# Rings of 8 and 12 slots, value products eleven tiles behind, tile 3 of each head transposed by DMA

## The chip, the cores and the metric

The kernel runs on one core of one Trainium2 chip. The metric is the device time of one execution in microseconds (us), from the first to the last instruction of the program with what the runtime puts around it. Three runs of the kernel before gave 1611.88, 1615.55 and 1622.05 us; the median, 1615.55 us, is the time to compare with.

## The reference

A conditioned transformer block on 2048 rows of 640 features: an attention part with 32 heads against a given K and V cache of 2048 rows per head, then a mixer and an MLP. Only the attention part is touched by the change.

```python
def _A_ref(x, k_cache, v_cache, wq, wo):            # x (1, 2048, 640), H, Dh = (32, 128)
    q = (x @ wq).reshape(B, Sq, H, Dh).transpose(0, 2, 1, 3)
    scores = jnp.einsum('bhqd,bhkd->bhqk', q, k_cache) * Dh ** (-0.5)
    p = _softmax(scores, axis=-1)
    o = jnp.einsum('bhqk,bhkd->bhqd', p, v_cache)
    return o.transpose(0, 2, 1, 3).reshape(B, Sq, H * Dh) @ wo
...
mod = (_silu(c) @ w_mod).reshape(c.shape[0], 6, 1, -1)
h = _layernorm(x, axis=-1) * (1 + ca) + sa
x = x + ga * _A_ref(h, A_k_cache, A_v_cache, A_wq, A_wo)
h = _layernorm(x, axis=-1) * (1 + cb) + sb
x = x + gb * _B_ref(h, B_w1, B_w2, B_w3, B_w4)
```

## The kernel before

A helper class records every operation with the keys that it reads and writes, works out the semaphore waits, and emits each engine's instructions in the order in which they were recorded. So every engine's queue is in order, and the order is written out by hand.

**The main loop** (lines 506 to 583) runs over steps `s`. There are `NG` = 512 tiles: 32 heads (`h`) of 16 tiles of 128 query rows (`j` is the tile within its head). In step `s` the engines are given this work:

- TensorE (PE): `qk(s, half)` (line 286), the scores of tile `s` against all 2048 keys, in two halves of two matmuls into the PSUM banks `Sps`; right behind each half, half of `pv(g_, half)` (line 299), the product of probabilities and values for tile `g_ = s - PVD`, eight tiles back. Further, one of the pieces of the next head's Q projection (`q_piece`, line 237), and, for tiles 3 and 10 of each head, a transpose of the probabilities on TensorE (`t_piece`, line 253: 4 transposes a half-step, 16 a tile).
- VectorE (DVE): line 546, twice a tile: it takes 1024 scores out of PSUM, scales them into `negS` (three slots) and keeps the row minimum. POOL joins the two minima (line 556).
- ScalarE (ACT): line 559, the exponential of all 2048 scores into slot `s % RP` of `Pb`, as bf16. It also copies finished outputs out of PSUM (line 537, once for two tiles), the Q pieces (line 244, four a head), and the transposed tiles of TensorE (`t_evac`, line 262; half of tile 3 goes through VectorE instead, line 264).
- SP issues the DMAs. `transpose(g, n)` (line 222) transposes one or two neighbouring tiles of `Pb` into `PTs`, where `pv` reads them as weights. A pair is taken where both tiles go by DMA, so the issues of a head are, by tile, (0,1), (2), (4,5), (6,7), (8,9), (11), (12,13), (14,15): fourteen tiles in eight DMAs. Between them on the same queue stand the next head's K (a transposing load, line 205, at `j == 2`), Wq (line 209, `j == 6`) and V (line 214, `j == PVD + 1` = 9).
- POOL normalises finished tiles `LAG` = 4 steps after their product (lines 440 and 447) and writes them to a scratch tensor in DRAM (line 454, once for four tiles).

`Pb` and `PTs` are the two halves of one tensor `ring` with 2 x `RP` = 20 slots of 128 x 2048 bf16 (512 KB each): 10 for the probabilities, 10 for their transposes. The exponential of tile `s` has to wait until the tile that last used its slot has been read (by its DMA or by TensorE), and a DMA transpose until its slot of `PTs` was read by `pv`.

Ahead of the loop stands a prologue (modulation, LayerNorm, the first Q). Behind it, the output projection, mixer and MLP (lines 584 to 801) reuse the same memory; the change does not alter their instructions.

Of the kernel before, what the change touches and what calls it, by code (L numbers as in the profile page):

```python
# [6 lines left out]
ACT = mybir.ActivationFunctionType  # L7
BF16 = mybir.dt.bfloat16
# [107 lines left out]
def bass_adaLN_cond__mha_block_cached__mixer_s_mlp__prompt_kernel(  # L116
    nc, A_x, A_k_cache, A_v_cache, A_wq, A_wo, B_x, B_w1, B_w2, B_w3, B_w4, c, w_mod, out,
):
    _, SQ, D = A_x.shape
    _, H, SK, DH = A_k_cache.shape  # L120
    FF = B_w3.shape[1]
    assert DH == 128 and D % 128 == 0 and SQ % 512 == 0 and SK == 2048
    KT = D // 128
    NQT = SQ // 128
    NQC = SQ // 512
    NKT = SK // 128
# [5 lines left out]
    NG = H * NQT  # L132
# [5 lines left out]
    with ExitStack() as es:  # L138
# [3 lines left out]
        ident = sb("ident", [128, 128], BF16)  # L142
# [7 lines left out]
        if True:  # L150
            with ExitStack() as es1:
                sb1 = lambda name, shape, dt: es1.enter_context(nc.sbuf_tensor(name, shape, dt))
                RP = 10
                PVD = 8
                PE_TILES = (3, 10)
                US = KT * (SQ + 4)
                sb1("pad", [128, 32], F32)
                ring = sb1("ring", [128, 2 * RP, SK], BF16)
                negS = sb1("negS", [128, 3, SK], F32)
                wo = sb1("wo", [128, H, D], BF16)  # L160
                kv = sb1("kv", [128, 2 * SK + 2 * NKT * 130 + 2 * KT * 128 + 2 * SQ], BF16)
# [7 lines left out]
                nm0, nm1, nm, rl = [small[:, 4 * NQT + 8 * i:4 * NQT + 8 * i + 8] for i in range(4)]  # L169
# [5 lines left out]
                Vaug = kv[:, o1:o2].rearrange("p (b k d) -> p b k d", b=2, k=NKT)  # L175
                wq = kv[:, o2:o3].rearrange("p (b k d) -> p b k d", b=2, k=KT)
                QT = kv[:, o3:o3 + 2 * SQ].rearrange("p (b q) -> p b q", b=2)
                Pb = ring[:, 0:RP]
                PTs = ring[:, RP:2 * RP].rearrange("p r (k q) -> p r k q", k=NKT)
                flat = ring[:].rearrange("p r s -> p (r s)")  # L180
                XO = SK
                x_sb = flat[:, XO:XO + NQT * D].rearrange("p (t d) -> p t d", t=NQT)
                WO_ = 6 * SK
                wmod = flat[:, WO_:WO_ + KT * 2 * D].rearrange("p (k n) -> p k n", k=KT)
                RO = 13 * SK
# [6 lines left out]
                CO = SO + NQT * 24  # L192
# [1 line left out]
                mcol = flat[:, CO + 2 * KT:CO + 6 * KT].bitcast(F32)  # L194
                c_sb = flat[:, CO + 6 * KT:CO + 7 * KT]
                s_col = flat[:, CO + 7 * KT:CO + 8 * KT]
                assert CO + 8 * KT <= 2 * RP * SK and XO + NQT * D <= WO_ and WO_ + KT * 2 * D <= 10 * SK
                PO = PTp[:].bitcast(F32)
                JB = [Oaug[:, 0:512], QPp[:, 0:512]]
                JBb = [Oaug[:].bitcast(BF16), QPb]  # L200
# [13 lines left out]
                    G.dma("sync", lambda e: e.dma_start(Vaug[:, hb, :, 0:128], A_v_cache[0, h].rearrange("(t p) d -> p t d", p=128)),  # L214
                          ("v", hb), w=[("V", hb)])

                assert RP % 2 == 0 and NQT % 2 == 0
                is_pe = lambda g: g % NQT in PE_TILES

                def transpose(g, n):  # L220
                    b = g % RP
                    G.dma("sync", lambda e: e.dma_start_transpose(
                        PTs[:, b:b + n].rearrange("p r k q -> p (r k) q"), ring[:, b:b + n].rearrange("p r s -> p (r s)")),
                        ("t", b), r=[("Pb", b + i) for i in range(n)], w=[("PT", b + i, z) for i in range(n) for z in range(2)])
                jbank = [0]
                bank_of = {}

# [19 lines left out]
                def t_piece(g, r, q):  # L247
                    jb = bank(("t", g, r))

                    def f(t):  # L250
                        for z in range(4 * q, 4 * q + 4):
                            kt = 8 * r + z
                            ins = t.transpose(JBb[jb][:, z * 128:(z + 1) * 128], Pb[:, g % RP, kt * 128:(kt + 1) * 128], ident[:])
                        return ins
                    G.op("tensor", f, r=[("Pb", g % RP)], w=[("J", jb)])

                def t_evac(g, r):
                    jb = bank(("t", g, r))
                    dst = PTs[:, g % RP, r * 8:(r + 1) * 8, :]
                    src = JBb[jb].rearrange("p (k q) -> p k q", k=8)  # L260
                    if not by_dve(g, r):
                        G.op("scalar", lambda a: a.copy(dst, src), r=[("J", jb)], w=[("PT", g % RP, r)])  # L262
                    else:
                        G.op("vector", lambda v: v.tensor_copy(dst, src), r=[("J", jb)], w=[("PT", g % RP, r)])

                by_dve = lambda g, r: r == 1 and g % NQT == PE_TILES[0]

                taken = [u for j in PE_TILES for u in range(2 * (j + 3), 2 * (j + 5))]
                QPIECE = {}
# [21 lines left out]

                def pv(g, half):
                    hb = (g // NQT) % 2
                    b = g % RP
                    ob = PO[:, ((g // 2) % 2) * 512 + (g % 2) * 130:]

                    def f(t):
                        for kt in range(half * 8, half * 8 + 8):
                            ins = t.matmul(ob[:, 0:129], PTs[:, b, kt, :], Vaug[:, hb, kt, 0:129],  # L299
                                           start=(kt == 0), stop=(kt == NKT - 1))  # L300
                        return ins
                    G.op("tensor", f, r=[("PT", b, half), ("V", hb), "ones"], w=[("O", (g // 2) % 2)])

                ringk = lambda a, b: [k for i in range(a // SK, -(-b // SK)) for k in (
                    [("Pb", i)] if i < RP else [("PT", i - RP, 0), ("PT", i - RP, 1)])]
                WMK = ringk(WO_, WO_ + KT * 2 * D)
                WRK = ringk(RO, 2 * RP * SK)
                XK = [ringk(XO + cc * 4 * D, XO + (cc + 1) * 4 * D) for cc in range(NQC)]

                def load_x(cc):  # L310
# [149 lines left out]
                XB0 = XT0 + NQT * D  # L460
                GT0 = XB0 + NQT * D * 2
                NFT4 = NFT * 512
                assert GT0 + NFT4 <= 2 * RP * SK
                tmp = flat[:, 0:4 * D].bitcast(F32).rearrange("p (b d) -> p b d", b=2)
                xt = flat[:, XT0:XT0 + NQT * D].rearrange("p (t d) -> p t d", t=NQT)
                xb = flat[:, XB0:XB0 + 2 * NQT * D].bitcast(F32).rearrange("p (t d) -> p t d", t=NQT)
# [36 lines left out]
                        + ringk(XT0 + 4 * cc * D, XT0 + 4 * (cc + 1) * D))  # L503

                LAG = 4
                for s in range(NG + PVD + LAG):
                    h, j = divmod(s, NQT)
                    g_ = s - PVD
                    evacs = []
                    if s <= 2:  # L510
                        for i in ((0,), (1, 2), range(3, len(MROW)))[s]:
# [5 lines left out]
                    for half in range(2):  # L517
                        if s < NG:
                            qk(s, half)
                        if 0 <= g_ < NG:  # L520
                            pv(g_, half)
                        if s == 0 and half == 1:
                            q_head0(NQC - 1)
                        if h + 1 < H and 2 * j + half in QPIECE:
                            cc, q = QPIECE[2 * j + half]
                            q_piece(h + 1, cc, q)
                            if q == KT - 1:
                                evacs.append((q_evac, h + 1, cc))
                        for r in range(2):
                            g = s - 3 - r  # L530
                            if 0 <= g < NG and is_pe(g):
                                t_piece(g, r, half)
                                if half == 1:
                                    evacs.append((t_evac, g, r))
                    if 0 <= g_ < NG and g_ % 2 == 1:
                        p = g_ // 2
                        G.op("scalar", lambda a, p=p: a.copy(  # L537
                            Of[:, p % 4].rearrange("p z d -> p (z d)")[:, 0:259], PO[:, (p % 2) * 512:(p % 2) * 512 + 259]),
                            r=[("O", p % 2)], w=[("Of", p % 4)])
# [15 lines left out]
                    if s < NG:  # L555
                        G.op("gpsimd", lambda g, r8=r8: g.tensor_scalar(  # L556
                            out=nm[:, r8:r8 + 1], in0=nm0[:, r8:r8 + 1], scalar1=nm1[:, r8:r8 + 1], scalar2=None, op0=ALU.min),
                            r=[("nmh", 0, r8), ("nmh", 1, r8)], w=[("nm", r8)])
                        G.op("scalar", lambda a, s=s, r8=r8: a.activation(  # L559
                            Pb[:, s % RP, :], negS[:, s % 3, :], ACT.Exp, bias=nm[:, r8:r8 + 1], scale=-1.0),  # L560
                            r=[("negS", s % 3), ("nm", r8)], w=[("Pb", s % RP)])
                        if not is_pe(s):
                            if s % 2 == 1 and not is_pe(s - 1):
                                transpose(s - 1, 2)
                            elif s % 2 == 1 or is_pe(s + 1):
                                transpose(s, 1)
                        if j == 2 and h >= 1 and h + 1 < H:
                            load_k(h + 1)
                        if j == 6 and h + 2 < H:
                            load_wq(h + 2)  # L570
                        if j == PVD + 1 and h + 1 < H:
                            load_v(h + 1)
                    if 0 <= s - PVD - LAG:
                        gr, z = divmod(s - PVD - LAG, 4)
                        if z == 0:
                            rcp(gr)
                        norm(gr, z)
                    if s == NG:
                        load_ot(0)
                        for cc in range(NQC):  # L580
                            load_xt(cc)
                    if s == NG + 1:
                        load_ot(1)
                GELU = ACT.Gelu_apprx_tanh
                YB = [Sps[:, 0:1024], Sps[:, 1024:2048]]
# [96 lines left out]
                for n in range(KT):  # L682
                    lst = []
                    p = 0
# [146 lines left out]
```

## Time and profile before

| | |
|---|---|
| median of three runs | 1615.55 us |
| the three runs | 1611.88, 1615.55, 1622.05 us |
| span of the profiled execution | 1613.0 us, 34611 instructions |
| VectorE line 546, 1024 of them | 1220 ns each |
| ScalarE line 559, 512 of them | 2017 ns each |
| DMA transposes `ring<-ring`, 256 of them | 7.0 us from issue to landing (median) |
| mean granted TensorE clock | 0.993 |

The main loop fills most of the span: in the trace VectorE's first instruction of line 546 starts at 35.7 us and its last ends at 1260.4 us, which is 1224.7 us for 32 heads. A mean duration in a table of groups is that of one instruction by itself; neighbours on an engine overlap a little (two of VectorE's line 546 start 1.14 us apart when nothing holds them up), so the pace is read from starts. Some records of DMA packets overlap as well, so that the share of the 16 DMA engines can be over 1 in a stretch in which they do nothing else. Of the profiled execution only its span is known; it lies 2.6 us below the median of the runs.

### The profile page before, as it was taken

What the parts mean: (1) busy time and instruction counts of PE and PEld (TensorE: products, weight loads), DVE (VectorE), ACT (ScalarE), POOL (GpSimd) and SP (SyncE); (2) the same over time, 40 slices, a digit from 0 to 9 for tenths busy, and PEclk for the clock granted to TensorE, in tenths of its full rate; (3) what the DMA queues carried; (4) which work ended last, traced back from release to release, by engine and by line L of the source; (5) the groups of instructions that cost most, each with busy time, mean ns of one, the idle gap of its engine ahead of it and who ended that gap; (6) DMA issues with size and microseconds to landing.
All of it is one profiled execution on the core that took longest, in us unless ns stands there. A gap on an engine that the chain in (4) does not pass through costs nothing.

```text
span 1613.0 us, 34611 instructions
## 1 busy us (share of the span) xinstructions
PE 1489.2 (92%) x13978; PEld 962.9 (60%) x14231; DVE 1394.3 (86%) x2460; ACT 1294.9 (80%) x1145; POOL 622.8 (39%) x1394
## 2 busy tenths in 40 slices
PE   5899999999999999999999999999999799999998
PEld 3466666666666666666666666666666555545444
DVE  6999999999999999999999999999999256665424
ACT  4999999999999999999999999999999300055330
POOL 0244444444444444444444444444444323222000
PEclk9999999999999999999999999999999799999999
DMA  9999999999999999999999999999999995530000
GB/s 305 231 230 234 243 238 235 241 242 242 233 243 236 244 232 242 238 235 238 242 249 229 245 237 233 245 237 233 241 237 245 214 213 105 105 111 1 17 17 34
DMA packets 1167728, 333.60 MB, mean 207 GB/s; under 512 B 1148304, under 2 KB 1161552, under 8 KB 1167568
## 3 DMA queue, kind: packets, MB, share of 16 engines
q1 hardware_dynamic: 1161424, 314.59, 97.5%
q0 software_dynamic: 6144, 16.79, 3.4%
q8 instruction: 112, 1.84, 0.5%
q14 instruction: 48, 0.39, 0.1%
HBM read 43.48 MB, written 19.40 MB: 39 GB/s over the span
## 4 chain that ended last, share of the span: by engine, by line
ACT 29%; DVE 24%; PE 21%; DMA 16%; issue 8%; POOL 2%; SPq 0%; POOLq 0%; DVEq 0%
ACT ring L559 23%; DVE negS L546 22%; DMA ring<-ring 13%; PE Sps L618 7%; PE Sps L759 4%; ACT ring L262 2%; PE Oaug L743 2%; PE QPp L743 2%; ACT Of L537 1%; ACT kv L244 1%; PE Sps L728 1%; PE PTp L299 1%; DMA ring<-in_A_x_dram 1%; POOL small L556 1%; PE Sps L286 1%
## 5 line engine op out<-in xcount | busy, mean ns | idle before, releaser
L546 DVE TENSOR_SCALAR_CACHE_REDUCE negS<-Sps 128x1024 f32<-128x1024 f32 x1024 | 1179.0, 1220 | 30.3 <-PE Sps L286 29.5
L559 ACT ACTIVATE ring<-negS,small 128x2048 bf16<-128x2048 f32 x512 | 1029.3, 2017 | 22.7 <-POOL small L556 20.5
L299 PEld LDWEIGHTS PTp<-kv,ring 128*128 128x128 bf16 x8192 | 553.0, 98 | 313.0 <-DMA ring<-ring 97.4
L299 PE MATMUL PTp<-kv,ring 128*128 128x129 bf16 x8192 | 647.9, 221 | 51.2 <-DMA ring<-ring 49.1
L286 PE MATMUL Sps<-kv 128*128 128x512 bf16 x1950 | 592.3, 381 | 35.6 <-DVE negS L546 18.1
L556 POOL TENSOR_SCALAR small<-small 128x1 f32<-128x1 f32 x512 | 145.9, 285 | 631.2 <-DVE negS L546 631.2
L286 PEld LDWEIGHTS Sps<-kv 128*128 128x128 bf16 x2048 | 144.7, 97 | 139.6 <-DVE negS L546 94.6
L447 POOL TENSOR_SCALAR On<-Of,small 128x128 bf16<-128x128 f32 x512 | 189.9, 371 | 13.4 <-DMA o_scratch<-On 0.5
L656 ACT COPY kv<-PTp 128x640 bf16<-128x640 bf16 x32 | 22.0, 692 | 154.8 <-PE PTp L653 154.8
L440 POOL TENSOR_TENSOR small<-Of,small 128x4 f32<-128x4 f32 x128 | 133.1, 1040 | 6.7 <-ACT Of L537 6.7
L454 POOL DMA_DIRECT2D o_scratch<-On x128 | 103.1, 806 | 40.8 <-POOL On L447 37.2
L537 ACT COPY Of<-PTp 128x259 f32<-128x259 f32 x256 | 95.7, 374 | 11.1 <-PE PTp L299 11.1
L237 PE MATMUL Oaug<-hTx,kv 128*128 128x512 bf16 x264 | 100.4, 385 | 3.9 <-DVE hTx L396 3.9
L237 PE MATMUL QPp<-hTx,kv 128*128 128x512 bf16 x259 | 97.7, 382 | 2.7 <-ACT hTx L391 2.2
L546 DVE DVE_READ_ACCUMULATOR negS<-Sps 128x1 f32 x1024 | 85.8, 84 | 0.0
L599 POOL TENSOR_SCALAR On<-On 128x1 f32<-128x1 f32 x48 | 24.3, 507 | 152.2 <-DVE On L608 152.2
L626 DVE TENSOR_TENSOR ring<-Sps,mod_bc 128x640 f32<-128x640 f32 x16 | 13.2, 824 | 77.6 <-PE Sps L618 77.6
L618 PE MATMUL Sps<-wo,hTx 128*128 128x128 bf16 (+1 forms) x504 | 71.2, 303 | 5.3 <-DMA hTx<-o_scratch 4.9
L618 PE MATMUL Sps<-wo,negS 128*128 128x128 bf16 (+1 forms) x504 | 69.1, 298 | 1.5 <-DMA negS<-o_scratch 1.1
L763 DVE TENSOR_TENSOR ring<-Sps,ring 128x640 f32<-128x640 f32 x16 | 13.2, 824 | 66.2 <-PE Sps L759 66.2
L262 ACT COPY ring<-Oaug 128x1024 bf16<-128x1024 bf16 x64 | 65.2, 1019 | 0.0
L618 PEld LDWEIGHTS Sps<-wo,hTx 128*128 128x128 bf16 x512 | 40.2, 99 | 36.6 <-DMA hTx<-o_scratch 4.8
(82 smaller groups left out, 1004.2 us busy)
## 6 DMA issues: line engine op xcount, KB each, us to landing
kv<-in_A_v_cache_dram SPq DMA_DIRECT2D x32, 512.0 KB, 5.0
o_scratch<-On POOLq DMA_DIRECT2D x128, 128.0 KB, 3.8
ring<-in_A_x_dram SPq DMA_DIRECT2D x8, 640.0 KB, 5.1
kv<-in_A_wq_dram SPq DMA_DIRECT2D x32, 160.0 KB, 3.4
wo<-in_A_wo_dram SPq DMA_DIRECT2D x1, 5120.0 KB, 16.5
ring<-ring SPq DMA_TRANSPOSE x256, 7.0
ring<-in_w_mod_dram SPq DMA_DIRECT2D x1, 3200.0 KB, 13.5
out_dram<-wo SPq DMA_DIRECT2D x16, 160.0 KB, 1.8
```

Of the source, the lines that this page charges most:

```text
L237: G.op("tensor", lambda t: t.matmul(JB[jb], wq[:, hb, q, :], hT[:, q, cc * 512:(cc + 1) * 512], start=(q == 0), stop=(q == KT - 1)), r=[(" ...
L262: G.op("scalar", lambda a: a.copy(dst, src), r=[("J", jb)], w=[("PT", g % RP, r)])
L286: ins = t.matmul(Sps[:, col:col + 512], QT[:, hb, j * 128:(j + 1) * 128], KTs[:, hb, col:col + 512], start=True, stop=True)
L299: ins = t.matmul(ob[:, 0:129], PTs[:, b, kt, :], Vaug[:, hb, kt, 0:129], start=(kt == 0), stop=(kt == NKT - 1))
L440: G.op("gpsimd", lambda g: g.tensor_tensor(out=rl[:, 4 * b:4 * b + 4], in0=Of[:].rearrange("p a z d -> p (a z) d")[:, 4 * b:4 * b + 4, 128 ...
L447: G.op("gpsimd", lambda g: g.tensor_scalar(out=On[:, b, z, :], in0=Of[:, 2 * b + z // 2, z % 2, 0:128], scalar1=rl[:, 4 * b + z:4 * b + z ...
L454: G.dma("gpsimd", lambda e: e.dma_start(o_scr[jj // 2:jj // 2 + 2, :, hh].rearrange("a p z d -> p a (z d)"), On[:, b].rearrange("p (a z) d ...
L537: G.op("scalar", lambda a, p=p: a.copy(Of[:, p % 4].rearrange("p z d -> p (z d)")[:, 0:259], PO[:, (p % 2) * 512:(p % 2) * 512 + 259]), r= ...
L546: G.op("vector", lambda v, half=half, s=s, r8=r8: v.tensor_scalar(out=negS[:, s % 3, half * 1024:(half + 1) * 1024], in0=Sps[:, half * 102 ...
L556: G.op("gpsimd", lambda g, r8=r8: g.tensor_scalar(out=nm[:, r8:r8 + 1], in0=nm0[:, r8:r8 + 1], scalar1=nm1[:, r8:r8 + 1], scalar2=None, op ...
L559: G.op("scalar", lambda a, s=s, r8=r8: a.activation(Pb[:, s % RP, :], negS[:, s % 3, :], ACT.Exp, bias=nm[:, r8:r8 + 1], scale=-1.0), r=[( ...
L618: ins = t.matmul(YB[b][:, c0:c0 + cw], OTj[pr % 2][:, 2 * hh + z, :], wo[:, hh, c0:c0 + cw], start=(hh == 0), stop=(hh == H - 1))
```

## The change

The number of slots stays 20, but 8 are now for the probabilities (`RPB`) and 12 for their transposes (`RPT`). The value products run eleven tiles behind (`PVD` = 11) instead of eight; over the last tiles of the last head the distance falls step by step from eleven to eight (`PVE`), with two products in some steps, so that the last product and what follows stand in the same steps as before. The load of V moves from `j == 9` to `j == 12` with `PVD`. Only tile 10 of each head is transposed on TensorE. Tile 3 goes by DMA: the eight DMAs of a head are then (0,1), (2,3), (4,5), (6,7), (8,9), (11), (12,13), (14,15), fifteen tiles; the DMA of tile 2 is issued in step 3 instead of 2, behind the load of K. The copy of half of tile 3 by VectorE and the one by ScalarE go with it, and the Q pieces, which keep clear of the steps with TensorE transposes, now lie in steps 0 to 9 of a head (before: 0 to 4 and 8 to 12).

```diff
-                RP = 10
-                PVD = 8
-                PE_TILES = (3, 10)
+                RPB, RPT = 8, 12
+                PVD, PVE = 11, 8
+                PE_TILES = (10,)
...
-                ring = sb1("ring", [128, 2 * RP, SK], BF16)
+                ring = sb1("ring", [128, RPB + RPT, SK], BF16)
...
-                    b = g % RP
+                    b, t = g % RPB, g % RPT
                     G.dma("sync", lambda e: e.dma_start_transpose(
-                        PTs[:, b:b + n].rearrange("p r k q -> p (r k) q"), ring[:, b:b + n].rearrange("p r s -> p (r s)")),
-                        ("t", b), r=[("Pb", b + i) for i in range(n)], w=[("PT", b + i, z) for i in range(n) for z in range(2)])
+                        PTs[:, t:t + n].rearrange("p r k q -> p (r k) q"), ring[:, b:b + n].rearrange("p r s -> p (r s)")),
+                        ("t", b), r=[("Pb", b + i) for i in range(n)], w=[("PT", t + i, z) for i in range(n) for z in range(2)])
...
-                by_dve = lambda g, r: r == 1 and g % NQT == PE_TILES[0]
+                by_dve = lambda g, r: False
...
                 LAG = 4
-                for s in range(NG + PVD + LAG):
+                PVS, at = {}, []
+                for g in range(NG):
+                    d = max(PVE, min(PVD, PVE + (NG - 12 - g) // 2))
+                    at.append(max(g + d, at[-1] if g else 0))
+                    PVS.setdefault(at[g], []).append(g)
+                assert all(len(v) <= 2 for v in PVS.values())
+                NORMS = {}
+                for g in range(NG):
+                    NORMS.setdefault(at[g] + LAG, []).append(g)
+                OT0 = max(NG, at[NG - NQT + 3] + LAG + 1)
+                for s in range(at[-1] + LAG + 1):
                     h, j = divmod(s, NQT)
-                    g_ = s - PVD
+                    pvs = PVS.get(s, [])
...
                         if s < NG:
                             qk(s, half)
-                        if 0 <= g_ < NG:
-                            pv(g_, half)
+                        for g_ in pvs:
+                            if len(pvs) == 1:
+                                pv(g_, half)
+                            elif g_ == pvs[half]:
+                                pv(g_, 0)
+                                pv(g_, 1)
...
                         G.op("scalar", lambda a, s=s, r8=r8: a.activation(
-                            Pb[:, s % RP, :], negS[:, s % 3, :], ACT.Exp, bias=nm[:, r8:r8 + 1], scale=-1.0),
-                            r=[("negS", s % 3), ("nm", r8)], w=[("Pb", s % RP)])
+                            Pb[:, s % RPB, :], negS[:, s % 3, :], ACT.Exp, bias=nm[:, r8:r8 + 1], scale=-1.0),
+                            r=[("negS", s % 3), ("nm", r8)], w=[("Pb", s % RPB)])
...
-                    if 0 <= s - PVD - LAG:
-                        gr, z = divmod(s - PVD - LAG, 4)
+                    for g_ in NORMS.get(s, []):
+                        gr, z = divmod(g_, 4)
...
-                    if s == NG:
+                    if s == OT0:
                         load_ot(0)
```

The remaining lines of the diff put `RPB` and `RPT` where `RP` stood (slots, keys and size checks), let the copies out of PSUM and the normalisation follow the new schedule of products, and take `OT0`, which comes out as 512 like `NG`, for the first load of the scratch tensor.

More of the change, by code (lines that the diff above doesn't have):

```diff
@@ L177, in bass_adaLN_cond__mha_block_cached__mixer_s_mlp__prompt_kernel @@
                 QT = kv[:, o3:o3 + 2 * SQ].rearrange("p (b q) -> p b q", b=2)
-                Pb = ring[:, 0:RP]
-                PTs = ring[:, RP:2 * RP].rearrange("p r (k q) -> p r k q", k=NKT)
+                Pb = ring[:, 0:RPB]
+                PTs = ring[:, RPB:RPB + RPT].rearrange("p r (k q) -> p r k q", k=NKT)
                 flat = ring[:].rearrange("p r s -> p (r s)")
@@ L196, in bass_adaLN_cond__mha_block_cached__mixer_s_mlp__prompt_kernel @@
                 s_col = flat[:, CO + 7 * KT:CO + 8 * KT]
-                assert CO + 8 * KT <= 2 * RP * SK and XO + NQT * D <= WO_ and WO_ + KT * 2 * D <= 10 * SK
+                assert CO + 8 * KT <= (RPB + RPT) * SK and XO + NQT * D <= WO_ and WO_ + KT * 2 * D <= 10 * SK
                 PO = PTp[:].bitcast(F32)
@@ L215, in load_v @@
                           ("v", hb), w=[("V", hb)])
-                assert RP % 2 == 0 and NQT % 2 == 0
+                assert RPB % 2 == 0 and RPT % 2 == 0 and NQT % 2 == 0
                 is_pe = lambda g: g % NQT in PE_TILES
                 def transpose(g, n):
-                    b = g % RP
+                    b, t = g % RPB, g % RPT
                     G.dma("sync", lambda e: e.dma_start_transpose(
-                        PTs[:, b:b + n].rearrange("p r k q -> p (r k) q"), ring[:, b:b + n].rearrange("p r s -> p (r s)")),
-                        ("t", b), r=[("Pb", b + i) for i in range(n)], w=[("PT", b + i, z) for i in range(n) for z in range(2)])
+                        PTs[:, t:t + n].rearrange("p r k q -> p (r k) q"), ring[:, b:b + n].rearrange("p r s -> p (r s)")),
+                        ("t", b), r=[("Pb", b + i) for i in range(n)], w=[("PT", t + i, z) for i in range(n) for z in range(2)])
                 jbank = [0]
@@ L252, in f @@
                             kt = 8 * r + z
-                            ins = t.transpose(JBb[jb][:, z * 128:(z + 1) * 128], Pb[:, g % RP, kt * 128:(kt + 1) * 128], ident[:])
+                            ins = t.transpose(JBb[jb][:, z * 128:(z + 1) * 128], Pb[:, g % RPB, kt * 128:(kt + 1) * 128], ident[:])
                         return ins
-                    G.op("tensor", f, r=[("Pb", g % RP)], w=[("J", jb)])
+                    G.op("tensor", f, r=[("Pb", g % RPB)], w=[("J", jb)])
                 def t_evac(g, r):
                     jb = bank(("t", g, r))
-                    dst = PTs[:, g % RP, r * 8:(r + 1) * 8, :]
+                    dst = PTs[:, g % RPT, r * 8:(r + 1) * 8, :]
                     src = JBb[jb].rearrange("p (k q) -> p k q", k=8)
                     if not by_dve(g, r):
-                        G.op("scalar", lambda a: a.copy(dst, src), r=[("J", jb)], w=[("PT", g % RP, r)])
+                        G.op("scalar", lambda a: a.copy(dst, src), r=[("J", jb)], w=[("PT", g % RPT, r)])
                     else:
-                        G.op("vector", lambda v: v.tensor_copy(dst, src), r=[("J", jb)], w=[("PT", g % RP, r)])
-                by_dve = lambda g, r: r == 1 and g % NQT == PE_TILES[0]
+                        G.op("vector", lambda v: v.tensor_copy(dst, src), r=[("J", jb)], w=[("PT", g % RPT, r)])
+                by_dve = lambda g, r: False
                 taken = [u for j in PE_TILES for u in range(2 * (j + 3), 2 * (j + 5))]
@@ L293, in pv @@
                     hb = (g // NQT) % 2
-                    b = g % RP
+                    b = g % RPT
                     ob = PO[:, ((g // 2) % 2) * 512 + (g % 2) * 130:]
@@ L304, in bass_adaLN_cond__mha_block_cached__mixer_s_mlp__prompt_kernel @@
                 ringk = lambda a, b: [k for i in range(a // SK, -(-b // SK)) for k in (
-                    [("Pb", i)] if i < RP else [("PT", i - RP, 0), ("PT", i - RP, 1)])]
+                    [("Pb", i)] if i < RPB else [("PT", i - RPB, 0), ("PT", i - RPB, 1)])]
                 WMK = ringk(WO_, WO_ + KT * 2 * D)
-                WRK = ringk(RO, 2 * RP * SK)
+                WRK = ringk(RO, (RPB + RPT) * SK)
                 XK = [ringk(XO + cc * 4 * D, XO + (cc + 1) * 4 * D) for cc in range(NQC)]
@@ L462, in bass_adaLN_cond__mha_block_cached__mixer_s_mlp__prompt_kernel @@
                 NFT4 = NFT * 512
-                assert GT0 + NFT4 <= 2 * RP * SK
+                assert GT0 + NFT4 <= (RPB + RPT) * SK
                 tmp = flat[:, 0:4 * D].bitcast(F32).rearrange("p (b d) -> p b d", b=2)
@@ L534, in bass_adaLN_cond__mha_block_cached__mixer_s_mlp__prompt_kernel @@
                                     evacs.append((t_evac, g, r))
-                    if 0 <= g_ < NG and g_ % 2 == 1:
-                        p = g_ // 2
+                    for p in [g_ // 2 for g_ in pvs if g_ % 2 == 1]:
                         G.op("scalar", lambda a, p=p: a.copy(
@@ L581, in bass_adaLN_cond__mha_block_cached__mixer_s_mlp__prompt_kernel @@
                             load_xt(cc)
-                    if s == NG + 1:
+                    if s == OT0 + 1:
                         load_ot(1)
```

## The prediction

> **What bounds the kernel now.** I read the page first (busy shares, slices), then the list of waits, the timeline of SP's queue, the chain of waits, and the busy time by stretches.
>
> ```profile
> PE 1489.2 (92%) x13978; PEld 962.9 (60%) x14231; DVE 1394.3 (86%) x2460; ACT 1294.9 (80%) x1145; POOL 622.8 (39%) x1394
> DMA  9999999999999999999999999999999995530000
> q1 hardware_dynamic: 1161424, 314.59, 97.5%
> ```
>
> The shares alone don't decide: TensorE, VectorE, ScalarE and the DMA engines are all nearly full in the main loop. The waits say who holds up whom (engine, line, what it waited for: us in total, times, longest):
>
> ```profile
> PEld PTp L299 <- DMA ring<-ring: 97.4, 105, 3.1
> PE PTp L299 <- DMA ring<-ring: 49.1, 70, 2.9
> DVE negS L546 <- PE Sps L286: 29.5, 45, 2.2
> ```
>
> TensorE stands before a value product until a DMA transpose has landed; behind that product the next `qk` is queued, and VectorE runs out of scores. So some transposes land too late. Is that latency, which a larger distance would cover, or throughput, which it would not? SP's queue tells (start, us, instruction; one head and the start of the next):
>
> ```profile
> 628.85 2.00 SPq L205 DMA_TRANSPOSE kv<-in_A_k_cache_dram  x1
> 630.90 4.70 SPq L222 DMA_TRANSPOSE ring<-ring  x1
> 635.65 0.58 SPq L209 DMA_DIRECT2D kv<-in_A_wq_dram  x1
> 636.27 9.42 SPq L222 DMA_TRANSPOSE ring<-ring  x2
> 645.74 0.59 SPq L214 DMA_DIRECT2D kv<-in_A_v_cache_dram  x1
> 646.37 21.31 SPq L222 DMA_TRANSPOSE ring<-ring  x5
> 667.73 2.20 SPq L205 DMA_TRANSPOSE kv<-in_A_k_cache_dram  x1
> 669.97 4.51 SPq L222 DMA_TRANSPOSE ring<-ring  x1
> ```
>
> Each issue starts 0.04 to 0.05 us after the last one ends: the queue is never empty. In head 0 that is different:
>
> ```profile
> 57.10 3.90 ACT L559 ACTIVATE ring<-negS,small 128x2048 bf16<-128x2048 f32 x2
> ...
> 61.03 9.12 SPq L222 DMA_TRANSPOSE ring<-ring  x2
> ```
>
> There the issue starts at 61.03, when its exponential ends (57.10 + 3.90 = 61.00). Counting exponentials and issues from the first, the issue for tiles (4,5) of head 16 at 669.97 belongs to an exponential that ended at 666.10: it started 3.9 us late. Over the run this lag is 0 in head 0, 1.7 us on average in head 1, 2.9 in head 2, and about 4 in heads 4 to 29; it is never below 1.7 in heads 2 to 30, and falls to 0 in head 31, where no K or V is loaded. So when VectorE sets the pace the backlog grows, until late products slow the rest down. (The list of SP's waits puts 613.4 us on a ScalarE copy, line 537; by this counting the data had been there for microseconds, so I don't follow it.) The chain of waits in head 16 agrees: it goes through DMA pieces of 8 to 9 us, then the product, `qk` and VectorE:
>
> ```profile
> 675.15 7.88 DMA ring<-ring
> 683.03 0.05 issue
> 683.08 0.64 PE PTp L299 x8
> ...
> 684.00 0.39 PE Sps L286
> ```
>
> The pace: VectorE's own is 32 starts of 1.143 us and one copy of 0.69 us, 37.3 us a head; head 1 (77.3 to 114.5) takes 37.2. Heads 2 to 30 (114.5 to 1222.9) take 1108.4 / 29 = 38.2 us, with the lag 2.7 us at their first issue and 2.2 behind their last. With the queue never empty, 38.2 us is what the DMA path needs for a head. The DMA engines agree (the last three columns: granted clock, DMA share, GB/s):
>
> ```profile
> 114.50:1222.90 1108.40, 1038.22 (x10595) 706.63 (x10788) 1084.29 (x1886) 1087.28 (x899) 505.65 (x1160) 1.00 1.21 239
> 595.00:598.00 3.00, 2.95 (x29) 1.93 (x28) 3.00 (x5) 2.97 (x3) 1.10 (x4) 1.00 1.27 290
> ```
>
> Transposes at their fullest move 290 GB/s at a share of 1.27; the average share of 1.21 is 95% of that.
>
> **The change, part by part.**
>
> *Tile 3 by DMA: removed.* VectorE loses a copy of 0.69 us a head (line 264), ScalarE one of about 0.91 us as spaced on its queue (1.02 recorded, line 262), TensorE 16 transposes, 4 x 0.27 = 1.1 us. VectorE's floor falls to 32 x 1.143 = 36.6 us a head, ScalarE's (16 x 1.90 exponentials, 8 x 0.26, 4 x 0.47 and now two copies of 0.91) to 36.2. Worth nothing while the DMA path needs 38.2; if that limit were gone, 1.6 us x 32 = 51 us.
>
> *Added.* One tile, 128 x 2048 x 2 B = 0.524 MB, in the same number of DMAs: the single (2) becomes the pair (2,3). Lowest bound: at 290 GB/s that is 1.81 us, less about 0.2 us if TensorE's 32 fewer instructions a head (of some 960) save a like share of the roughly 5 us a head in which packets stand still around code loads (an estimate: the records of 256 B packets over 0.1 us, added up over the engines): 1.6. Highest: SP's rows. The shortest issue of one tile takes 1.66 us, that of a pair about 4.0 (2.3 more); in heads 2 to 30 pairs start 4.7 us and the single (2) 2.2 us before the next issue, 2.5 more. Below 1.6, the only reserve is the 5% in which the engines aren't full, 1.9 us a head; but the gaps lie at fixed places (behind the wq load, around code loads), with the queue full behind them, so I take them to stay. I take 1.9, nearest to the byte rate, because in the full stretches packets follow one another without gaps, which makes the engines and not SP's issuing the limit.
>
> *Rule weighed.* The Trainium skill (Advanced Engine Details and Errata, X-Bar Transpose (TRN2)) holds DMA transposes to be as fast as plain DMAs, 350 to 400 GB/s. By it a tile would cost an estimated 1.3 to 1.5 us and the engines would have plenty of room. The trace disagrees: 290 GB/s in its fullest stretch.
>
> *Products eleven behind.* This moves each `pv` three steps, 3 x 2.29 = 6.9 us, and so lets the lag grow before TensorE waits. It adds no wait: V's load moves with it and finds its last reader done, as SP comes there some 4 us late. It costs nothing where the DMA path is the limit and gains its backlog once, not per head. The tail is unchanged, as the last products stand in the same steps.
>
> *Eight slots of `Pb`.* The exponential of tile `s` must find the pair (`s`-8, `s`-7) landed. From the end of exponential `s`-7 six others fit in: 6 x 2.4 = 14.3 us. An issue lands 7.0 us after it starts, so the new wait begins at a lag of about 7 us, before TensorE's at about 11. When it comes, ScalarE stands with its copies (lines 244, 537) behind it, and then VectorE, whose `negS` has three slots. But three further pairs are then already queued, so SP never runs dry, and the wait only passes on the DMA limit. Cost 0; if that cover failed, the rival below.
>
> *Twelve slots of `PTs`; Q pieces in steps 0 to 9.* A transpose into slot g mod 12 follows products that stood a step earlier or more: 0. A half-step with a Q piece takes TensorE 1.12 us against VectorE's 1.144, so twenty in a row leave little to catch up with, but at 38 us and more a head TensorE isn't the limit: 0.
>
> *Sum.* Heads 1 to 30 are DMA-limited: 30 x 1.9 = 57 us. Less 3 us, as the lag may grow from 4 to 7 us before anything waits; less 1 for head 31, which loads no K or V and runs at VectorE's pace. +53 on the profiled span: 1613 + 53 = 1666. The median is 2.6 us above that span: 1668. The bounds give 30 x 1.6 - 4 = +44 and 30 x 2.5 - 3 = +72: 1660 to 1688.
>
> **The rivals.**
>
> 1. *The DMA path has room, and lateness was latency (faster).* Then eleven tiles cover it and VectorE sets 36.6 to 37.0 us a head: 32 x 1.2 to 1.6 = 38 to 51 us less, about 1570. It decides if a head with fifteen tiles takes the DMA path under 37.8 us. For it: heads 19, 25, 26 and 30 ran at 37.3 to 37.6 us with the lag falling. The rule of the Trainium skill weighed above (Advanced Engine Details and Errata, X-Bar Transpose) would make it so, as by it there is room. Against: the lag grew from 0 whenever VectorE wasn't held up, and the average of 29 heads is 38.2 with fourteen tiles. 8%.
> 2. *The gaps take the tile.* 38.2 x 1.21/1.27 + 1.81 = 38.2 us a head, so 1613 to 1625 us. For it: larger rings smooth what jitter there is. Against: SP's queue was already full at each gap. 9%.
> 3. *Eight slots starve SP (slower still).* If ScalarE's wait for `Pb` kept exponentials back until SP had nothing queued, a pair's 7.0 us to landing would come into the path of some pairs, for one 2 us bubble a head more: 1668 + 60 = about 1730. Against: three pairs are queued. 3%.
>
> That tile 3 might still go through TensorE is excluded by the list `PE_TILES`.
>
> **How the numbers follow.** The forecast has 80%, the rivals 8, 9 and 3. A difference under 1% (16 us) can't be told from none here. Faster by over 1%: rival 1, 8%. Within 1%: rival 2, 9%. Slower: 83%. The range goes from 1630, between rival 2 and the lowest sum, as part of the gaps may be filled, to 1692, just over the highest sum. It leaves out rivals 1, 2 and 3.
>
> **What the new profile would show.** Right: SP's queue without a gap, heads of about 40 us, DMA share near 1.21 or above, ScalarE (line 559) newly waiting for DMA, VectorE idle 3 us a head. Wrong: issues that start with their exponential (SP idle), heads under 37.5 us, VectorE without idle time. The sum would be wrong in size if a head took 39.8 or 40.7 us: those are the two prices of a tile.

## The result and the profile after

The changed kernel takes 1671.88 us (median of four runs, 1667.53 to 1677.33) against 1615.24 us for the kernel before (median of four): a ratio of 1.0352, 95% interval 1.0324 to 1.0379, so 56.6 us more. The profiled execution has a span of 1672.7 us (its time was 1674.55 us). In the changed file the lines behind the loop's head have moved: VectorE's scores are now line 559, ScalarE's exponential 572, its copy of the outputs 550.

The busy shares of the engines fell, and that of the DMA queue rose (page, parts 1 and 3):

```profile
PE 1493.9 (89%) x13474; PEld 935.0 (56%) x13719; DVE 1382.0 (83%) x2428; ACT 1265.8 (76%) x1113; POOL 623.2 (37%) x1394
q1 hardware_dynamic: 1226960, 331.36, 99.2%
```

The list of waits (us in total, times, longest) has a new one among its largest, ScalarE's exponential behind a DMA transpose, and with it one of VectorE for ScalarE. Picked from the list:

```profile
ACT ring L572 <- DMA ring<-ring: 103.1, 81, 3.7
...
DVE negS L559 <- ACT ring L572: 75.8, 78, 3.5
...
PEld PTp L299 <- DMA ring<-ring: 25.0, 27, 3.8
...
PE PTp L299 <- DMA ring<-ring: 14.7, 14, 3.6
```

TensorE's wait for transposes shrank from 49.1 to 14.7 us (97.4 to 25.0 for its weight loads). In its place ScalarE waits for a slot of `Pb` that a DMA has yet to read, and VectorE waits for ScalarE. One head of SP's queue (start, us, instruction) still has no gap:

```profile
613.62 2.40 SPq L205 DMA_TRANSPOSE kv<-in_A_k_cache_dram  x1
616.06 8.95 SPq L222 DMA_TRANSPOSE ring<-ring  x2
625.06 0.59 SPq L209 DMA_DIRECT2D kv<-in_A_wq_dram  x1
625.69 10.95 SPq L222 DMA_TRANSPOSE ring<-ring  x3
636.68 0.59 SPq L214 DMA_DIRECT2D kv<-in_A_v_cache_dram  x1
637.31 15.10 SPq L222 DMA_TRANSPOSE ring<-ring  x3
652.45 3.06 SPq L205 DMA_TRANSPOSE kv<-in_A_k_cache_dram  x1
```

The stretches show both halves of the story. Heads 1 and 2 (76.6 to 113.2 to 149.8) run at VectorE's new floor, 36.6 us each with VectorE busy throughout; in them the backlog builds up. From there to head 31, 28 heads take 1131.4 us, 40.4 each (last three columns: granted clock, DMA share, GB/s):

```profile
76.60:113.20 36.60, 35.15 (x352) 23.30 (x356) 36.60 (x67) 36.38 (x31) 17.58 (x40) 1.00 1.19 235
...
149.80:1281.20 1131.40, 1009.34 (x9791) 657.74 (x9971) 1036.49 (x1794) 1023.78 (x841) 488.85 (x1121) 0.99 1.22 239
```

The same stretch before, 38.2 us a head, had a share of 1.21 and the same 239 GB/s:

```profile
152.00:1222.90 1070.90, 1002.53 (x10230) 682.41 (x10416) 1046.98 (x1821) 1049.92 (x868) 488.21 (x1120) 1.00 1.21 239
```

On average the DMA engines moved bytes no faster and no slower; there were more of them. In the chain of waits they now have the largest share (37% of the span, 16% before), with ScalarE's exponentials released by them:

```profile
694.72 7.08 DMA ring<-ring
701.80 0.02 issue
701.82 0.02 ACTq L101
701.84 0.04 issue
701.88 3.90 ACT ring L572 x2
```

### The profile page after: what moved, and what is told of

Read it like the earlier page. It is cut to its first block, busy times and chain, and to the rows that moved or that the text cites. A ratio compares the mean times of both kernels' runs of the same rounds, so it can differ in the third digit from the quotient of the medians.

```text
span 1672.7 us, 33785 instructions
## 1 busy us (share of the span) xinstructions
PE 1493.9 (89%) x13474; PEld 935.0 (56%) x13719; DVE 1382.0 (83%) x2428; ACT 1265.8 (76%) x1113; POOL 623.2 (37%) x1394
## 4 chain that ended last, share of the span: by engine, by line
DMA 37%; ACT 29%; PE 19%; DVE 8%; issue 5%; POOL 1%; SPq 0%; ACTq 0%; DVEq 0%; POOLq 0%
DMA ring<-ring 35%; ACT ring L572 23%; PE Sps L631 7%; DVE negS L559 7%; PE Sps L772 4%; ACT ring L262 2%; PE Oaug L756 2%; PE QPp L756 2%; ACT Of L550 2%; ACT kv L244 1%; PE Sps L741 1%; DMA ring<-in_A_x_dram 1%; DVE ring L364 1%; DMA negS<-o_scratch 1%; PE Sps L286 1%
## 5 line engine op out<-in xcount | busy, mean ns | idle before, releaser
L572 ACT ACTIVATE ring<-negS,small 128x2048 bf16<-128x2048 f32 x512 | 1012.3, 2009 | 114.6 <-DMA ring<-ring 103.1
L299 PEld LDWEIGHTS PTp<-kv,ring 128*128 128x128 bf16 x8192 | 562.1, 98 | 259.3 <-DMA ring<-ring 25.0
L286 PE MATMUL Sps<-kv 128*128 128x512 bf16 x1963 | 602.6, 385 | 102.4 <-DVE negS L559 78.3
L299 PE MATMUL PTp<-kv,ring 128*128 128x129 bf16 x8192 | 649.2, 222 | 15.0 <-DMA ring<-ring 14.7
L286 PEld LDWEIGHTS Sps<-kv 128*128 128x128 bf16 x2048 | 122.9, 97 | 252.6 <-DVE negS L559 216.8
L454 POOL DMA_DIRECT2D o_scratch<-On x128 | 103.1, 806 | 40.8 <-POOL On L447 37.2
L631 PEld LDWEIGHTS Sps<-wo,hTx 128*128 128x128 bf16 x512 | 40.1, 99 | 36.3 <-DMA hTx<-o_scratch 4.8
L631 PEld LDWEIGHTS Sps<-wo,negS 128*128 128x128 bf16 x512 | 39.6, 98 | 31.2 <-DMA negS<-o_scratch 1.0
```

The source lines that it names most:

```text
L286: ins = t.matmul(Sps[:, col:col + 512], QT[:, hb, j * 128:(j + 1) * 128], KTs[:, hb, col:col + 512], start=True, stop=True)
L454: G.dma("gpsimd", lambda e: e.dma_start(o_scr[jj // 2:jj // 2 + 2, :, hh].rearrange("a p z d -> p a (z d)"), On[:, b].rearrange("p (a z) d ...
L572: G.op("scalar", lambda a, s=s, r8=r8: a.activation(Pb[:, s % RPB, :], negS[:, s % 3, :], ACT.Exp, bias=nm[:, r8:r8 + 1], scale=-1.0), r=[ ...
L631: ins = t.matmul(YB[b][:, c0:c0 + cw], OTj[pr % 2][:, 2 * hh + z, :], wo[:, hh, c0:c0 + cw], start=(hh == 0), stop=(hh == H - 1))
```

## The experiments

Theory 1 is the prediction's: what the DMA path can carry in a head sets the pace (1a: bytes through the engines; 1b: SP's issuing). Theory 2: the eight slots for the probabilities cost the time. Theory 3: lateness was only latency. All head times below are means over heads 3 to 30 of one profiled execution, from the first instruction of VectorE's scores (line 559; 546 in the kernel before) in head 3 to the first in head 31. Each ratio is against the kernel before as timed in the same session; its median there lay between 1615.0 and 1618.5 us.

### Each half of the change alone

The rings and the distance alone, an edit of the changed kernel:

```diff
-                PE_TILES = (10,)
+                PE_TILES = (3, 10)
...
-                by_dve = lambda g, r: False
+                by_dve = lambda g, r: r == 1 and g % NQT == PE_TILES[0]
```

> The rings of 8 and 12 slots and the distance of eleven tiles, but tile 3 stays on TensorE as before (fourteen tiles a head by DMA). Theory 1, DMA throughput is the limit: the bytes of a head are those of before, so heads take 38.2 us again; the larger lag is gained once (about 3 us) and mostly given back in the tail: 1608 to 1618 us. Theory 2, the eight slots for the probabilities cost the time (ScalarE's new wait for DMA): 1655 to 1672 us. Theory 3, lateness was latency: 1570 to 1590 us.

Measured: 1609.55 us, ratio to the kernel before 0.9968 (0.9950 to 0.9986); 38.06 us a head.

Tile 3 alone, the reverse two lines in the kernel before:

> Tile 3 by DMA, but rings of 10 and 10 slots and products eight tiles behind as before. Theory 1, DMA throughput: heads of 40.2 to 40.5 us, 1668 to 1682 us, with TensorE instead of ScalarE waiting for DMA. Theory 2, the eight slots: this kernel has ten, so 1565 to 1620 us.

Measured: 1676.5 us, ratio 1.0362 (1.0329 to 1.0395); 40.0 us a head. Its waits are those of before, grown, and its list has no wait of ScalarE for DMA:

```profile
PEld PTp L299 <- DMA ring<-ring: 160.3, 114, 5.4
...
PE PTp L299 <- DMA ring<-ring: 107.4, 85, 5.2
...
DVE negS L546 <- PE Sps L286: 97.5, 86, 4.2
```

The four kernels make a table (medians, us; the one at the bottom right was timed in another session than the other three, in which the kernel before took 1615.2):

| | tile 3 on TensorE | tile 3 by DMA | difference |
|---|---|---|---|
| rings 10 and 10, eight behind | 1615.0 | 1676.5 | +61.5 |
| rings 8 and 12, eleven behind | 1609.6 | 1671.9 | +62.3 |
| difference | -5.4 | -4.6 | |

Within what these runs can tell, the two halves add up. Tile 3 costs about 62 us with either pair of rings. The rings gain 5.5 us with tile 3 on TensorE (the interval reaches from 2.3 to 8.1); the 4.6 us with tile 3 by DMA is less than the spread of either kernel's runs and stands for nothing by itself. Theory 2 falls: with ten slots the time is no shorter, and only the place of the wait changes (TensorE there, ScalarE here). Theory 3 falls too: with eleven tiles of distance and no more bytes than before, many heads run at VectorE's 37.2 us (heads 1 to 4, 20 to 26), but the mean stays 38.06. What the DMA path needs isn't the same in every head, though: from head 20 to head 27 the lag of the issue for tiles (0,1) grew by 2.0 us, 0.3 a head, so that there 37.5 us were enough.

### Bytes taken away

```diff
-                        if j == PVD + 1 and h + 1 < H:
+                        if j == PVD + 1 and h == 0:
                             load_v(h + 1)
```

> The changed kernel without the loads of V from head 2 on (the products use the V of heads 0 and 1). That takes 0.52 MB a head, as much as one tile, off the DMA engines. Theory 1a, bytes through the DMA engines are the limit: heads fall from 40.4 by 2.2 us, 30 heads, to 1600 to 1612 us. Theory 1b, SP's issuing is the limit: V holds SP for 0.63 us a head, so 19 us less, about 1653 us. Theory 2, the eight slots: no change, 1665 to 1675 us.

Measured: 1604.87 us (ratio 0.9932, 0.9907 to 0.9956), 67 us less than the changed kernel; 37.9 us a head:

```profile
149.80:1210.20 1060.40, 993.45 (x9791) 652.49 (x9971) 1031.15 (x1795) 1019.05 (x839) 490.19 (x1121) 1.00 1.22 241
```

That is theory 1a's size, 2.5 us a head, and four times what V holds SP. The eight slots are still there. By the records V goes through SP's queue in packets of 256 B, as a tile does (some 2050 fewer a head in this run), so the run doesn't part bytes from packets. With K's load gone as well (`if j == 2 and h >= 1 and h + 1 < H` becomes `if False`):

> The changed kernel without the loads of V and of K from head 2 on (they use those of heads 0 and 1): two tiles' worth of bytes a head less. Theory 1: the DMA path then needs about 36 us a head, under VectorE's floor of 36.6, so heads of 36.6 to 37 us, 1555 to 1575 us: that is where the time is that the change takes off VectorE, ScalarE and TensorE. Theory 2, the eight slots or the distance: over 1600 us.

Measured: 1567.61 us (ratio 0.9686, 0.9660 to 0.9712), every head from 1 to 30 at 36.62 us, VectorE busy for 1049.92 of 1050 us:

```profile
150.00:1200.00 1050.00, 1032.66 (x10200) 665.41 (x10198) 1049.92 (x1836) 1043.65 (x858) 499.86 (x1147) 1.00 1.18 235
```

This is the floor that the change uncovers, and it can't be held while the DMA path has a tile's worth more to carry (37.9 us with K, above). The rings, the distance and the Q pieces packed into steps 0 to 9 all stand in this kernel, and VectorE doesn't wait for them.

### The same bytes from other queues

V from head 1 on issued by POOL:

```diff
-                    G.dma("sync", lambda e: e.dma_start(Vaug[:, hb, :, 0:128], ...
-                          ("v", hb), w=[("V", hb)])
+                    G.dma("sync" if h == 0 else "gpsimd", lambda e: e.dma_start(Vaug[:, hb, :, 0:128], ...
+                          ("v" if h == 0 else "vp", hb), w=[("V", hb)])
```

> The changed kernel with the loads of V from head 1 on issued by POOL instead of SP: the same bytes, another queue. Theory 1a, bytes through the DMA engines: 1655 to 1680 us (the lower end if POOL's queue moves larger packets). Theory 1b, SP's issuing: 0.63 us a head off SP's queue, about 1650 us or less.

Measured: 1772.67 to 1815.7 us in four runs, 100 us and more above the changed kernel and far from both. In six heads ScalarE waited 9 to 18 us for a transpose behind V's load. Stretches of 4 us behind one such load, issued at 354.2 us:

```profile
356.00:360.00 4.00, 3.29 (x40) 2.41 (x38) 3.31 (x7) 2.98 (x3) 1.78 (x5) 1.00 1.30 143
360.00:364.00 4.00, 3.00 (x24) 1.61 (x24) 3.58 (x7) 3.01 (x3) 1.95 (x4) 1.00 1.39 72
364.00:368.00 4.00, 0.00 (x0) 0.00 (x0) 0.33 (x2) 0.00 (x0) 0.65 (x2) 0.85 1.37 48
368.00:372.00 4.00, 0.00 (x0) 0.00 (x0) 0.00 (x0) 0.00 (x0) 0.00 (x0) 0.50 1.35 51
```

The share stays at 1.30 or more while the rate falls to 50 GB/s: the engines' packets last long and move little (between 360 and 372 us up to 4.5 us for one of V, 1.9 us for one of a transpose; half of all 256 B packets in the loop before take 0.018 us or less). From POOL's queue V comes in packets of 4096 B, and in the trace they lie in time among the 256 B packets of the transposes, from 360 to 376 us one among some 17. The Trainium skill (DMA: Bandwidth & Descriptors, Queues, rings and completion order) says that a DMA engine takes turns between the queues that have work, a packet of several descriptors at a time. The records here name a packet's queue but not its engine, so they don't show such turns, and why the mixture is so slow no run here shows. As a test of 1a against 1b this run tells nothing, as it changed the size of V's packets too. I took from it a new theory, 1c: other queues' packets hold up the transposes in the kernel before and after too, through POOL's four writes of finished tiles a head. So those went to SP:

```diff
-                    G.dma("gpsimd", lambda e: e.dma_start(
+                    G.dma("sync", lambda e: e.dma_start(
                         o_scr[jj // 2:jj // 2 + 2, :, hh].rearrange("a p z d -> p a (z d)"),
```

> The changed kernel with its finished tiles written to the scratch tensor from SP's queue instead of POOL's: the same bytes, but no packets of a second queue in the main loop apart from code loads. In the run with V on POOL the DMA engines fell to about 50 GB/s for some 16 us while packets of 4096 B of the second queue lay between those of the transposes. Theory 1c, such packets hold up the transposes, and are part of why a tile costs 2.2 us instead of the 1.81 us of the fullest stretches: four writes a head, 0.3 to 0.8 us each, so heads of 37.5 to 39.2 us and 1575 to 1640 us. Theory 1a, bytes alone count: 40 to 41 us a head, 1660 to 1690 us. Theory 1b, SP's issuing is the limit: four more issues of 0.63 us, 2.5 us a head longer, about 1750 us.

> The same move of the writes to SP, in the kernel with the new rings and distance but tile 3 on TensorE. Theory 1c: the DMA path needs less than VectorE's 37.2 us a head, so VectorE sets the pace: 1580 to 1592 us. Theory 1a: 38.1 us a head as in that kernel without the move, 1605 to 1620 us. Theory 1b: about 1690 us.

Measured: 1704.46 us (ratio 1.0534, 1.0510 to 1.0559) and 1643.6 us (1.0162, 1.0135 to 1.0189): each about 30 us more than without the move by the ratios, 0.9 and 1.1 us a head. Theory 1c, which forecast a gain, gets no support: with the writes gone from POOL's queue the loop's rate didn't rise (234 GB/s from 150 to 1200 us in both). The size lies between 1a and 1b, and the runs can't part them, or say what the writes cost on POOL's queue, as they bring a wait of their own. SP's late queue makes the writes late, POOL waits for its buffers, and the row minimum that ScalarE needs stands behind that on POOL:

```profile
POOL On L447 <- DMA o_scratch<-On: 399.4, 121, 27.1
...
ACT ring L572 <- POOL small L569: 140.6, 87, 4.1
```

### Tiles moved the other way

If the DMA path is the limit, more tiles on TensorE should help until another engine is the limit. Edit of the kernel with the new rings alone, for every fourth, second, or every head (here 4):

```diff
-                is_pe = lambda g: g % NQT in PE_TILES
+                is_pe = lambda g: g % NQT in PE_TILES or (g % NQT == 11 and (g // NQT) % 4 == 3)
...
-                by_dve = lambda g, r: r == 1 and g % NQT == PE_TILES[0]
+                by_dve = lambda g, r: r == 1 and g % NQT in (3, 11)
...
-                taken = [u for j in PE_TILES for u in range(2 * (j + 3), 2 * (j + 5))]
+                taken = [u for j in (3, 10, 11) for u in range(2 * (j + 3), 2 * (j + 5))]
```

The last line keeps the Q pieces clear of the steps in which tile 11 is transposed.

> The other way round: the new rings and distance, tiles 3 and 10 on TensorE, and in every fourth head tile 11 too (its second half copied out by VectorE). Theory 1 at 2.2 us a tile: the DMA path falls from 38.1 by 0.55 to 37.5 us a head on average, VectorE and ScalarE rise by about 0.2 to 37.4: about 1594 to 1600 us. If the DMA path were not the limit: 1610 us or more, as VectorE and ScalarE only get more work.

> The same in every second head. Theory 1: the DMA path at 37.0, VectorE and ScalarE at 37.6 us a head, so they set the pace: 1593 to 1602 us. Otherwise: over 1610 us.

> The same in every head. Theory 1: the DMA path at 35.9, ScalarE and VectorE at 38.0 us a head: 1603 to 1615 us, SP's issues starting soon after their exponentials again.

Measured: 1609.96, 1627.42 and 1669.81 us; ratios 0.9961 (0.9943 to 0.9979), 1.0077 (1.0062 to 1.0092) and 1.0342 (1.0324 to 1.0359). All three miss theory 1's ranges, and the times alone fit the other expectation as well; the heads tell more. With thirteen tiles in every head the backlog is gone, as theory 1 says: the issues of tiles (0,1), (12,13) and (14,15) start within 0.2 us of their exponential's end in heads 3 to 30, and the DMA rate falls to 216 GB/s. But the heads take 39.87 us, not 38.0: the transposes of tiles 10 and 11 fall into one step, and the two PSUM banks that they share with the Q pieces wait for copies. The chain of waits at that step, and the wait that belongs to it:

```profile
632.51 1.86 ACT ring L572
634.37 0.18 issue
634.55 1.04 ACT ring L262
635.60 0.05 issue
635.64 0.40 PE QPp L253 x4
636.04 0.45 PE Sps L286 x2
636.49 0.02 issue
636.51 1.23 DVE negS L559 x2
```

```profile
PEld Oaug L253 <- ACT ring L262: 45.4, 32, 1.6
```

A transposed half waits in its bank behind an exponential, the next transposes wait for the bank, and the scores behind them on TensorE wait too. The head is 2.65 us longer than VectorE's 37.22; 0.6 of it is VectorE's copy for tile 11 (a step with its other copy takes 2.89 us instead of 2.29), and some 2.0 us are the clash. In the kernel with every fourth head, the others but head 0 run at 37.2 us, all 23, where the kernel without the third tile had a mean of 38.06: so the relief works. The eight relieved heads take 39.9 to 42.6 and give it back.

To get rid of that clash I put tiles 4 and 11 on TensorE, and 13 as well in every fourth head, so that the transposes of tile 11 fall in steps 14 and 15 and those of tile 13 in steps 0 and 1 of the next head, with the Q pieces in the steps between:

```diff
-                PE_TILES = (3, 10)
+                PE_TILES = (4, 11)
...
-                is_pe = lambda g: g % NQT in PE_TILES
+                is_pe = lambda g: g % NQT in PE_TILES or (g % NQT == 13 and (g // NQT) % 4 == 2)
...
-                by_dve = lambda g, r: r == 1 and g % NQT == PE_TILES[0]
+                by_dve = lambda g, r: r == 1 and g % NQT in (4, 13)
...
-                taken = [u for j in PE_TILES for u in range(2 * (j + 3), 2 * (j + 5))]
+                taken = [u % (2 * NQT) for j in (4, 11, 13) for u in range(2 * (j + 3), 2 * (j + 5))]
```

> The new rings and distance, with tiles 4 and 11 of each head on TensorE (fourteen tiles a head by DMA), and in every fourth head tile 13 too, three steps from its neighbours, so that the transposes of two tiles never fall in one step as tiles 10 and 11 did. Theory 1: the DMA path's backlog, at 38.1 us a head, is worked off in every fourth head, so that three heads of four run at VectorE's floor of 37.2 us and the fourth at 38.0 or less: 37.4 on average, 1588 to 1597 us. If the fourth head still clashes: about 1610 us.

> The control without the third tile: fourteen tiles a head by DMA as in the kernel with tiles 3 and 10. Theory 1: the DMA path sets 38.0 to 38.2 us a head after the first few heads, 1606 to 1616 us.

Measured: 1608.21 us (0.9959, 0.9944 to 0.9975) and, for the control, 1611.42 us (0.9979, 0.9965 to 0.9993). The control is as expected, the other is not: 38.07 us a head, where 37.4 was forecast. The third tile does work the backlog off (the issue behind it starts 0 to 3 us late), but its two copies come in steps 0 and 1 of the next head and lengthen steps 0 to 2 from 2.29 to as much as 3.1, 3.4 and 2.5 us: 0.6 to 2.2 us in heads 3 to 27, 1.6 on average, most of what the DMA path would have taken for it. That explains 11 of the 24 us by which heads 3 to 30 exceed 37.22 us each. The other 13 lie in heads with fourteen tiles, up to 40.1 us long; ScalarE still waited 15.7 us for transposes (23.2 in the control). Three kernels thus stand 0.3 to 0.4% below the kernel before, and their intervals overlap; none is clearly better than another.

## Why the prediction was right, and what was off

The forecast was 1668 us, measured are 1671.88, a miss of 4 us. That it is so small is partly luck: on the profiled spans the forecast was 1666 and the measurement 1672.7, and the profiled execution happened to be 2.7 us slower than the median of its kernel. (In every run on record the time is 1.7 to 1.9 us more than the span, so most of the 2.6 us that the forecast added to the span is this distance.)

**What bounds the kernel** was read rightly: SP's queue without a gap and a lag that grew from 0 meant that the DMA path was already full with fourteen tiles. The two halves apart, and V and K taken away, show it.

**Removed work worth nothing.** Right: the changed kernel runs at VectorE's floor of 36.6 us in heads 1 and 2 alone, while the backlog builds up; once K and V are gone, all of heads 1 to 30 do.

**The price of a tile: "I take 1.9, nearest to the byte rate".** Somewhat low: a head got 40.41 - 38.25 = 2.16 us longer, which contains the small gain of the rings. The medians of the table give 61.5 and 62.3 us over 30 heads, 2.05 to 2.08 a head; single executions scatter (1.8 and 2.3 for the two pairs). I priced the tile at the 290 GB/s of the fullest stretch. By the DMA records of heads 3 to 30, the 2 us behind the start of each code-load record take 7.9 us a head before and after, and the engines move 139 GB/s in them before and 130 after; in the rest of a head they move 265 GB/s both times. So the gaps around code loads did stay, as I had taken them to; the tile went through at 265 GB/s, which makes 1.98 us, and the slower stretches behind code loads are left with the other 0.2. Both bounds, 1.6 and 2.5, held.

**Eight slots, cost 0; eleven behind, a gain once.** Right in mechanism: ScalarE's new wait appeared and TensorE's shrank. The slots let the lag grow further than "about 7 us": for tiles (2,3) to (8,9) it is 9 to 10. The rings and the distance together gained 5.5 us with tile 3 on TensorE; the interval, 2.3 to 8.1, doesn't exclude the 3 of the sum.

**Head 31 "runs at VectorE's pace", -1.** Wrong: it took 40.4 us, against 37.5 before. The larger backlog is worked off there: the lag is still 5.5 to 6 us up to tiles (8,9) and 0.5 at the last issue, where before it had gone from 2.2 to 0. On the profiled executions the loop's sum is -0.6 (head 0), -1.4 (heads 1 and 2), +60.5 (heads 3 to 30), +2.9 (head 31) = +61.4, and the whole span grew by 59.7 (the part behind the loop was 1.7 us shorter), where 53 was forecast. The medians differ by 56.6.

**The rivals.** That the path has room, and that gaps take the tile, are both refuted by the table; the starved SP of the third didn't come, as SP's queue has no gap over 0.5 us between 150 and 1170 us. The Trainium skill's rule from the prediction (Advanced Engine Details and Errata, X-Bar Transpose (TRN2)), 350 to 400 GB/s for transposes, isn't borne out here either: the mean stayed at 239.

## What to carry to other kernels

When an issuing queue has no gap and its issues start later and later behind their data, the path behind it is probably full, and more distance or slots then only move the wait, as they did here; see whether the lag grows while the other engines run freely, and take bytes away to make sure. Price an addition to a full path at its rate over whole periods, not at the rate of its best stretch. Where several resources lie within 1 us of each other in a period of 38 (here the DMA path at 38.2, VectorE at 37.2, ScalarE not far below), moving work among them gains little, and the floor that a change uncovers is a gain only if the next resource has room.

## What the runs showed of the hardware that I had not expected

Loads of 0.5 MB in 4096 B packets from POOL's queue, beside DMA transposes from SP's, brought the DMA engines from 239 GB/s on average to about 50 for some 12 us in the worst case looked at (364 to 376 us), and the kernel from 1671.88 to 1772.67 us and more. POOL's writes of 128 KB, four a head, stand in the kernels before and after, and no 4 us of heads 3 to 30 fall under 75 GB/s there.

The mean rate of 239 GB/s in the loop was the same with fourteen and fifteen tiles a head, though 290 are reached for microseconds. A large part of the difference lies around code loads: 130 to 139 GB/s in the 2 us behind the start of each code-load record, 265 elsewhere. No run here changed the code loads, so whether they are the cause stays open.
